# A forgetting attention and a bilinear FFN on one core: the order of issue, the engines of the casts and the buffers laid out anew

## The chip, the core and the metric

The program runs on one core of a Trainium2 chip. A core has five engines with a queue each: PE (TensorE, the matmuls, with its weight loads shown apart as PEld), DVE (VectorE), ACT (ScalarE), POOL (GpSimd) and SP (SyncE, which here only issues transfers). Each engine runs its own list in order and waits by semaphore for what it reads and for the buffers that it writes; 16 DMA engines move what SP, ACT and POOL issue. The metric is the device time of one execution in microseconds. A lower number is better.

## The reference: what is computed

An attention with a decay between tokens, over 8 batches of 8 heads with 576 tokens and 64 features, and then an FFN in which two projections are multiplied:

```python
scores = scale * np.matmul(q, k.transpose(0, 1, 3, 2))
log_f = np.log(np.clip(f, 0.0001, 1.0))
cum = np.cumsum(log_f, axis=-1)
decay = cum[:, :, :, None] - cum[:, :, None, :]
scores = np.where(causal, -1000000000.0, scores + decay)
scores = scores - np.max(scores, axis=-1, keepdims=True)
attn = np.exp(scores)
attn = attn / (np.sum(attn, axis=-1, keepdims=True) + 1e-09)
...
x = np.ascontiguousarray(attn_out.transpose(0, 2, 1, 3)).reshape(B * S, H * D)
...
a = x @ w_a
b = x @ w_b
return (a * b @ w_out).astype(np.float32)
```

All inputs and the output are float32 in DRAM; the kernel multiplies in float16.

## The kernel before

Two heads make a pair, so that there are 32 pairs t, four to a batch. The queries of a pair are cut into blocks i of 128 rows (four, and a last one of 64). For each pair the kernel does this:

- q and k are loaded in halves of a batch (`load_qk`, L339 on SP for batches 1 to 7 into three float32 buffers `n32`, and L334 on POOL's queue for batch 0, where the transfer itself makes float16), cast to float16 (`cast_qk`, lines 291 and 293 on POOL after batch 0), transposed on PE (`pe_transpose`, L359, PSUM tile psT) and copied out to qT and kT (`pe_evict`). v is loaded at L305 (POOL, batches 0 and 1, straight into nv) or L300 (SP, then cast).
- The cumulated logarithm of f is worked out once at the start: two clips (L225, columns 0 to 255 and 256 to 575), two logarithms on ACT (L260), two scans (L228), two casts into a float16 table `crow` (L264), and the low part that float16 loses (`low_part`, L233), one subtraction for each half of the heads. The sums are also stored to DRAM (L238), from where later pairs load them spread over all partitions (L625).
- Scores are matmuls into PSUM tiles sc. In batch 0 the decay is added by matmuls with `crow`, and a row maximum is taken (L646); later it is added on DVE in one pass with the maximum (L674, into S). ACT takes the exponential with its sum (L701, L705, into PA for the blocks 0 to 2 and PB for the rest), DVE the reciprocal (L715 and L713), and POOL or ACT multiplies the rows by it (the normalisation, L726).
- The probabilities are transposed, on PE for batch 0 and partly batch 1 (PSUM tile psP), else by a DMA transpose that SP issues (`do_tr`, L740, PTA from PA and PTB from PB). The product with v (PSUM pv, or pvx from batch 2 on) is copied to xT, the FFN's input.

The FFN takes the tokens in pieces of 256 (three), 384, 512 (six) and 384. A piece is 12 blocks of the inner dimension: matmuls into psa (with w_a) and psb (with w_b), ACT copies psa out to float16, DVE multiplies it with psb into ht (L1073), and for each 128 tokens 24 matmuls with w_out give pso, which ACT or DVE copies to osb and SP stores (L1116). The weights come by POOL's queue (L510): w_a and w_b in a first third and the rest, each in two halves of the partitions, and w_out in three parts. 24 `wake` blocks of matmuls without a use are strewn over the opening.

Nothing schedules this at run time or when it is built. The functions only make a list of 2353 steps (`Op`, with engine, dependencies and the rings of buffers that they take); the long table `ORDER` says in which order the steps are issued, and so the list of each engine; `CHOICE` has one letter for each step that may run on several engines (casts, copies out of PSUM, normalisations), and `SLOTS` says which buffer of its ring each allocation takes. The dependencies of a step become waits on semaphores. Each engine takes its steps strictly in this order, so that a step that waits holds all that stand behind it. Rings around the change: three buffers `n32` for loads, two S, four PA, two PB, three PTA, two PTB, four PSUM banks `ff` (psa, psb, pso, psT, psP, pv) and two `sc` pairs.

Of the kernel before, what the change touches and what calls it, by code (L numbers as in the profile page):

```python
# [25 lines left out]
def kernel(  # L26
# [13 lines left out]
    B, H, S, D = q.shape  # L40
# [22 lines left out]
    qd = [perm.tile([128, 128], FP16, tag=f"qd{i}", name=f"qd{i}") for i in range(2)]  # L63
# [41 lines left out]
    def paddings():  # L105
# [14 lines left out]
    nv = [perm.tile([128, NSB, H, D], FP16, tag=f"nv{i}", name=f"nv{i}") for i in range(2)]  # L120
# [21 lines left out]
        PA:03210213021302130213021302130213;PB:01101010101010101010101010101010;S:010110100110100110101011001101  # L142
        01010101001010101010101010010011010100101001000100010011011010011100111011010101110101;a16:0210210210210
        21021021021021021021201201210210210210201201201012012021021021020120120201010201210201201201201201021;bc
        :0210210210210210210210210210;ff:03120312032100023120310323231232301230103010103203013120312031203120312
        03123012310120213203203013203210312013201320130123021312312031232013012013023103210131310321320312031023
        10210321032130230231023102312302130213021321023023012032032031310210210312310231302132013203210310231023
        20120210102120321312012013203103021301321301302102302310230132031203120132013012012021023101301321032132
        030231031031032031230123201230312312312312312312302311021021302301231231230;ht:0dcba981234567d0bc9a18234
        5670dbc9a182543d670cb9a1428653d70cb2a9154863d7bac025914863dcb7a9205148dc36a9b72051483cdb6;n16:0110100101  # L150
        10001010010101010101;n32:0210201201201201020101212110210220201212202101;nv:01010101;osb:0101010101001010
        10101010010100110101;qd:010101010101010101010101;sc:0101010101010101010101011010010101100010101011001001
        0101101010101011010101010101010100101011101100101010110101100101100100101010;st:054321503421503421503421
        50342150
# [1054 lines left out]
    for n in cuts:  # L1209
# [3 lines left out]
        0 1 29 30 46 2 52 62 5 3 31 37 32 38 33-36 39 40 42 41 53 47 58 4 43 267 262 279 6-9 54 48 10 56  # L1213
# [160 lines left out]
```

## Time and profile before

| what | us |
|---|---|
| median of three runs | 400.78 |
| the three runs | 397.33, 400.78, 401.96 |
| span of the profiled execution | 397.5 |

The profiled execution's span lies by the fastest of the three runs. All times from the trace count from the start of this span. The page lists for each engine its busy time; a window row gives the busy time of each engine within a stretch; a timeline row gives start, length, engine, line, operation, tiles and shapes, and in brackets the idle time ahead of it with what ended it. Idle time of an engine that is not the bottleneck costs nothing by itself.

### The profile page before, as it was taken

What the parts mean: (1) busy time and instruction counts of PE and PEld (TensorE: products, weight loads), DVE (VectorE), ACT (ScalarE), POOL (GpSimd) and SP (SyncE); (2) the same over time, 40 slices, a digit from 0 to 9 for tenths busy, and PEclk for the clock granted to TensorE, in tenths of its full rate; (3) what the DMA queues carried; (4) which work ended last, traced back from release to release, by engine and by line L of the source; (5) the groups of instructions that cost most, each with busy time, mean ns of one, the idle gap of its engine ahead of it and who ended that gap; (6) DMA issues with size and microseconds to landing.
All of it is one profiled execution on the core that took longest, in us unless ns stands there. A gap on an engine that the chain in (4) does not pass through costs nothing.

```text
span 397.5 us, 14691 instructions
## 1 busy us (share of the span) xinstructions
PE 386.4 (97%) x5768; PEld 250.9 (63%) x5768; DVE 293.0 (74%) x971; ACT 290.6 (73%) x805; POOL 257.8 (65%) x464
## 2 busy tenths in 40 slices
PE   6899999999999999999999999999999999999997
PEld 3557887969766665655555665555555556567785
DVE  7888798999998779787888798668878772333131
ACT  5999899999879778778988588898878763232131
POOL 8689687769887679884996877779936871000000
PEclk9999999999999999999999999999999999999999
DMA  7999999999999999999999999999999586100202
GB/s 117 256 195 167 157 147 226 220 285 283 244 188 228 238 293 234 235 249 292 231 205 278 223 255 214 248 258 206 252 220 230 104 147 156 63 2 1 81 28 81
DMA packets 147365, 76.87 MB, mean 193 GB/s; under 512 B 124384, under 2 KB 128352, under 8 KB 147296
## 3 DMA queue, kind: packets, MB, share of 16 engines
q1 hardware_dynamic: 132856, 68.72, 77.7%
q0 software_dynamic: 14256, 7.08, 14.7%
q8 instruction: 45, 0.74, 0.8%
q14 instruction: 24, 0.20, 0.2%
q10 hardware_dynamic: 184, 0.14, 0.1%
HBM read 52.05 MB, written 9.58 MB: 155 GB/s over the span
## 4 chain that ended last, share of the span: by engine, by line
PE 77%; DMA 11%; POOL 4%; ACT 3%; issue 2%; DVE 2%; SPq 0%; DVEq 0%; ACTq 0%; POOLq 0%
PE psa L74 21%; PE psb L74 20%; PE pso L74 20%; PE sc L551 4%; DMA PTA<-PA 3%; PE pvx L769 3%; POOL PA L726 2%; DMA PTB<-PB 2%; PE psT L359 2%; DMA wb<-in_moe_w_b_dram 2%; PE sc L539 2%; DMA wout<-in_q_dram 2%; PE sc L74 1%; PE psP L74 1%; DMA k<-in_k_dram 1%
## 5 line engine op out<-in xcount | busy, mean ns | idle before, releaser
L674 DVE CUSTOM_DVE_ANT_0 S<-sc,spread 64x576 f32<-64x576 f32 (+4 forms) x232 | 125.9, 562 | 17.3 <-ACT PA L705 8.3
L74 PE MATMUL psb<-xT,wb 128*64 128x512 f16 (+2 forms) x1056 | 113.9, 341 | 0.8 <-DMA wb<-in_moe_w_b_dram 0.5
L74 PE MATMUL psa<-xT,wa 128*64 128x512 f16 (+2 forms) x1056 | 114.1, 341 | 0.0
L289 ACT CAST a<-psa 128x512 f16<-128x512 f32 (+1 forms) x114 | 63.3, 559 | 56.4 <-PE psa L74 52.3
L1073 DVE TENSOR_TENSOR ht<-psb,a 128x512 f16<-128x512 f32 (+1 forms) x114 | 74.4, 658 | 38.5 <-PE psb L74 27.7
L74 PE MATMUL pso<-wout,ht 128*64 128x512 f16 x840 | 102.4, 380 | 0.0
L726 POOL TENSOR_SCALAR PA<-PA,st 128x256 f16<-128x256 f16 (+2 forms) x180 | 84.9, 483 | 8.8 <-DVE st L715 5.5
L705 ACT ACTIVATE PA<-S,st 128x256 f16<-128x256 f32 (+2 forms) x168 | 84.2, 504 | 6.5 <-DVE st L674 6.0
L74 PEld LDWEIGHTS <-wb 128*64 128x64 f16 x1056 | 62.5, 110 | 30.0 <-issue 2.5
L74 PEld LDWEIGHTS <-wa 128*64 128x64 f16 x1056 | 61.7, 110 | 29.3 <-issue 2.2
L726 POOL TENSOR_SCALAR PB<-PB,st 128x512 f16<-128x512 f16 (+1 forms) x90 | 63.4, 711 | 24.3 <-DVE st L715 10.7
L74 PEld LDWEIGHTS <-ht 128*64 128x64 f16 x912 | 49.9, 110 | 33.0 <-issue 1.9
L705 ACT ACTIVATE PB<-S,st 128x512 f16<-128x512 f32 x56 | 40.2, 720 | 3.3 <-DVE st L674 3.0
L705 ACT ACTIVATION_READ_ACCUMULATOR PA<-S,st 128x1 f32 x168 | 32.1, 191 | 0.0
L701 ACT ACTIVATE PB<-S,st 128x576 f16<-128x576 f32 x28 | 21.7, 775 | 9.8 <-POOL PA L726 3.1
L631 POOL TENSOR_SCALAR_AFFINE_SELECT spread<-spread 128x768 f32<-128x768 f32 x24 | 20.9, 870 | 10.1 <-DMA spread<-cum_d 10.0
L769 PEld LDWEIGHTS <-nv 128*64 128x64 f16 x640 | 21.7, 110 | 7.5 <-DMA PTA<-PA 2.1
L674 DVE CUSTOM_DVE_ANT_1 S<-sc,spread 128x256 f32<-128x256 f32 x48 | 19.8, 419 | 6.9 <-PE sc L539 2.0
L715 DVE RECIPROCAL st<-st 128x2 f32<-128x2 f32 x128 | 18.3, 156 | 6.9 <-ACT PB L705 3.5
L674 DVE DVE_READ_ACCUMULATOR2_ANT st<- 128x1 f32 (+1 forms) x280 | 23.0, 82 | 0.0
L551 PE MATMUL sc<-kT,qT 64*128 64x512 f16 (+4 forms) x144 | 20.8, 326 | 1.2 <-ACT kT L289 0.4
L289 ACT COPY osb<-pso 128x512 f32<-128x512 f32 x24 | 13.8, 580 | 9.1 <-PE pso L74 7.8
(106 smaller groups left out, 483.2 us busy)
## 6 DMA issues: line engine op xcount, KB each, us to landing
spread<-cum_d SPq DMA_DIRECT2D x24, 576.0 KB, 6.4
out_dram<-osb SPq DMA_DIRECT2D x35, 256.0 KB, 3.4
q<-in_q_dram SPq DMA_DIRECT2D x14, 576.0 KB, 5.7
k<-in_k_dram SPq DMA_DIRECT2D x14, 576.0 KB, 5.0
v<-in_v_dram SPq DMA_DIRECT2D x24, 256.0 KB, 6.0
wout<-in_moe_w_out_dram POOLq DMA_DIRECT2D x3, 512.0 KB, 7.5
nv<-in_v_dram POOLq DMA_DIRECT2D x8, 128.0 KB, 5.1
wa<-in_moe_w_a_dram POOLq DMA_DIRECT2D x2, 512.0 KB, 7.5
```

What stands on the lines that cost most here:

```text
L74: nc.tensor.matmul(out=out[r], lhsT=lhsT[:, r], rhs=rhs, **kw)
L289: nc.scalar.copy(out=out_, in_=in_)
L359: nc.tensor.matmul(out=p[m][HP[j] if quad else slice(0, 128), 64 * t:64 * t + 64], lhsT=x[r, j, t, :] if quad else x[r, t, :], rhs=ident16 ...
L551: nc.tensor.matmul(out=dst, lhsT=lhsT, rhs=rhs, start=start, stop=stop, skip_group_check=True)
L631: nc.gpsimd.affine_select(out=c[:, :, 0:SM].rearrange("p h (j k) -> p h j k", k=128), in_=c[:, :, SM:2 * SM].rearrange("p h (j k) -> p h j ...
L674: nc.vector.tensor_tensor_reduce(out=o, in0=x, in1=y, scale=-1.0, scalar=3e38, op0=ADD, op1=MIN, accum_out=m)
L701: nc.scalar.activation(out=p_blocks(t, 4), in_=T[("s" if direct else "z", t, 4)], func=EXP, bias=st[:, 8:9], scale=sign, accum_out=st[:, 1 ...
L705: nc.scalar.activation(out=p_blocks(t, i)[:, :, h, :], in_=(T[("s", t, i)][:, h, :] if direct else T[("z", t, i)][:, h * n:h * n + n]).rea ...
L715: nc.vector.reciprocal(out=st[:, 20 + 2 * i:22 + 2 * i], in_=st[:, 10 + 2 * i:12 + 2 * i])
L726: VEC[e].tensor_scalar(out=p, in0=p, scalar1=st[:, c:c + 1], scalar2=1.0, op0=MUL, op1=MUL)
L769: nc.tensor.matmul(out=o[HP[h], 128 * i:128 * i + 128], lhsT=vt[:, j, pr + NP * h, :], rhs=pt[:, base_blk[i] + 2 * block_at(t, i, j) + h, ...
L1073: nc.vector.tensor_tensor(out=ht[:, 0:n_], in0=T.pop(("psb", t0, fbs))[:, 0:n_], in1=T.pop(("a16", t0, fbs))[:, 0:n_], op=MUL)
```

## The change

Only the three tables are replaced; the functions that make the steps, the 2353 steps and their dependencies stay. The core of the difference, a line or two of each table:

```diff
     SLOTS = """
-        PA:03210213021302130213021302130213;PB:01101010101010101010101010101010;S:010110100110100110101011001101
+        PA:01230321032103210321032103210321;PB:01101010101010101010101010101010;S:01010110101010101010101100110
...
     ORDER = """
-        0 1 29 30 46 2 52 62 5 3 31 37 32 38 33-36 39 40 42 41 53 47 58 4 43 267 262 279 6-9 54 48 10 56
+        46 2 0 1 29 3 37 31 52 62 5-8 30 38 9 10 32 44 54 56 48 50 33 34 36 35 11 63 53 64 47 4 82 55 65 57 39
...
     CHOICE = """
-        DDDDADADADAAPPAPPPAPPAADAPPPPPPAPADDDDPPPAPPPPPDDDDPAAPAPPPADDDADAADAAAADDPPPAPAPPPADDAAPPAP
+        DDPPADAAADAAPPPPAPPPPDDDDAPPPAPAPPADDDPPPPAPPPPDADAPAPPPAPPPDDDDAAAADAADDPPPPPPPPADDDDAAPAAPPAPAAAAPAA
```

By `CHOICE`, 12 normalisations move from ACT to POOL and nine from POOL to ACT, 11 copies of pso from ACT to DVE and three back, nine copies of psT from DVE to ACT and five back, and the low-part subtractions of the later 320 columns from DVE to POOL.

The list of DVE at the start, where f is prepared, as a piece of the difference (cum_f is f and then the sum, crow the float16 table):

```order
 L93 COPY pick_69<-ident_70 32x32
+L225 TENSOR_SCALAR cum_f<-cum_f 96x320
 L225 TENSOR_SCALAR cum_f<-cum_f 96x256
-L225 TENSOR_SCALAR cum_f<-cum_f 96x320
 L228 SCALAR_TENSOR_TENSOR cum_f<-cum_f,cum_l 96x256
```

The clip of the 320 columns stands first now.

The list of POOL ahead of the paddings, as a piece of the difference (low and neg are masks, wout holds the second half of k of batch 0 for a while, qd is padding):

```order
 L102 AFFINE_SELECT low_62<-low_62 64x128
+L334 DMA wout_78<-in_k_dram 128x2x576
+L233 TENSOR_TENSOR crow<-cum_f,crow 32x320 x2
 L107 MEMSET qd_63 128x128
 L107 MEMSET qd_64 128x128
```

The load of that half of k now follows the masks, and the two subtractions, which DVE did, follow it.

The list of POOL from the last memset of the opening on, before (PA holds probabilities, st the reciprocals, nv is v, spread the spread sums):

```order
L113 MEMSET nv_80 64x512
L726 TENSOR_SCALAR PA<-PA,st 128x128
L621 MEMSET spread_84 128x2x64
L305 DMA nv_79<-in_v_dram 128x8x64 x2
L291 TENSOR_SCALAR q_470<-q_184 128x2x9x64
L726 TENSOR_SCALAR PA<-PA,st 128x2x128
L293 CAST k_473<-k_186 128x2x9x64
```

and now, from the same memset on:

```order
L113 MEMSET nv_80 64x512
L305 DMA nv_79<-in_v_dram 128x8x64 x2
L621 MEMSET spread_84 128x2x64
L305 DMA nv_79<-in_v_dram 128x8x64
L510 DMA wb_77<-in_moe_w_b_dram 64x4x512 x2
L510 DMA wa_76<-in_moe_w_a_dram 64x4x512
L305 DMA nv_79<-in_v_dram 64x8x64
L510 DMA wa_76<-in_moe_w_a_dram 64x4x512
L726 TENSOR_SCALAR PA<-PA,st 128x128
L726 TENSOR_SCALAR PA<-PA,st 128x3x128
L621 MEMSET spread_85 128x2x64
L293 CAST k_554<-k_517 128x2x9x64
```

Four issues of v and four of weights have moved ahead of the first normalisation; the casts of batch 1 stand behind it.

The list of SP at the start, as a piece of the difference (k and q are the float32 loads of batches 1 and 2):

```order
 L213 DMA cum_f<-in_f_dram 32x1x576
+L339 DMA k_517<-in_k_dram 128x2x576
 L238 DMA cum_d<-cum_f 32x576 x2
-L339 DMA q_184<-in_q_dram 128x2x576
-L339 DMA k_186<-in_k_dram 128x2x576
-L339 DMA q_188<-in_q_dram 128x2x576
-L339 DMA k_618<-in_k_dram 128x2x576
-L339 DMA q_620<-in_q_dram 128x2x576
+L339 DMA q_584<-in_q_dram 128x2x576
+L339 DMA q_1096<-in_q_dram 128x2x576
```

The first k load of batch 1 now stands ahead of the store of the sums, and does not wait for them.

The list of POOL further on, around the cast of the first q half of batch 2, which was `q_1303` and is now `q_1653` to `q_1697`; before:

```order
L305 DMA nv_79<-in_v_dram 128x8x64
L291 TENSOR_SCALAR q_1303<-q_620 128x2x9x64
L305 DMA nv_79<-in_v_dram 128x8x64
L305 DMA nv_79<-in_v_dram 64x8x64
L726 TENSOR_SCALAR PB_83<-PB_83,st 128x4x128
```

and now:

```order
L305 DMA nv_80<-in_v_dram 128x8x64
L726 TENSOR_SCALAR PA<-PA,st 128x3x128 x2
L726 TENSOR_SCALAR PA<-PA,st 128x128
L291 TENSOR_SCALAR q_1697<-q_1653 128x2x9x64
L726 TENSOR_SCALAR PB_83<-PB_83,st 128x4x128 x2
L726 TENSOR_SCALAR PA<-PA,st 128x128 x2
L291 TENSOR_SCALAR q_1805<-q_1657 128x2x9x64
```

The cast has moved behind the loads of batch 1's v and the normalisations of pairs 3 to 5.

79 lines of the change are left out of this document (50 added, 29 removed), and 161 rows, old and new, of the table ORDER.

## The prediction

> **What bounds the kernel now.** I read the page first, then the windows by stage, then the list of TensorE's waits, then the timelines of the opening on each engine. The page says that TensorE is the bound:
>
> ```profile
> span 397.5 us, 14691 instructions
> PE 386.4 (97%) x5768; PEld 250.9 (63%) x5768; DVE 293.0 (74%) x971; ACT 290.6 (73%) x805; POOL 257.8 (65%) x464
> ```
>
> TensorE idles 397.5 - 386.4 = 11.1 us in all. The windows (us: TensorE, weight loads, VectorE, ScalarE, GpSimd, then clock, DMA share, GB/s) split the run at the first FFN matmul and at three later points:
>
> ```profile
> 0.00:35.60 35.60, 29.94 (x544) 17.69 (x544) 29.56 (x76) 28.34 (x83) 29.48 (x62) 1.00 0.98 187
> 35.60:121.00 85.40, 84.63 (x1692) 67.33 (x1688) 76.98 (x271) 78.31 (x216) 66.51 (x111) 1.00 1.17 217
> 121.00:175.00 54.00, 52.40 (x748) 33.45 (x744) 44.44 (x160) 43.47 (x127) 43.94 (x78) 1.00 1.14 238
> 175.00:340.00 165.00, 165.00 (x2204) 93.39 (x2202) 124.18 (x440) 125.67 (x352) 117.82 (x216) 1.00 1.02 220
> 340.00:397.50 57.50, 54.47 (x600) 39.05 (x596) 17.80 (x29) 14.80 (x29) 0.00 (x0) 1.00 0.12 43
> ```
>
> The idle time is 5.66 us before the FFN starts, 0.77 us from there to 121 us, 1.60 us to 175 us, none to 340 us, and 3.03 us at the end (the last copy and store). The clock is full throughout. So the time is about: the moment of the first FFN matmul, plus a fixed amount of matmuls, plus some 2.4 us of waits, plus a tail of 3 us. TensorE's waits, longest first:
>
> ```profile
> PE wake L74 <- POOL ident masks.py:199: 2.8, 1, 2.8
> PE pvx L769 <- DMA PTA<-PA: 1.3, 3, 0.8
> PE psT L359 <- DMA wout<-in_q_dram: 0.8, 1, 0.8
> PE psb L74 <- DMA wb<-in_moe_w_b_dram: 0.5, 1, 0.5
> ```
>
> The first is the start of the program. The third is in the opening: q of the second half lands late. The fourth is the second half of w_b, and the second the transposed probabilities of a pair. In the timeline of TensorE, the first FFN matmul, the two places of the later waits, and three transposes of q and k that the steps below need (39.84 and 42.90 of batch 1, 61.70 of batch 2) are these:
>
> ```profile
> 34.13 0.34 PE L769 MATMUL pv<-xT,nv 128*64 128x128 f16 x6
> 34.40 0.39 PE L551 MATMUL sc<-kT,qT 64*128 64x512 f16 x2
> 35.63 1.06 PE L74 MATMUL psa<-xT,wa 128*64 128x256 f16 x16
> 39.84 0.43 PE L359 MATMUL psT<-ident,q 64*128 64x64 f16 x18
> 42.90 0.44 PE L359 MATMUL psT<-ident,k 64*128 64x64 f16 x18
> 45.27 1.06 PE L74 MATMUL psb<-xT,wb 128*64 128x256 f16 x16 [0.46 <-DMA wb<-in_moe_w_b_dram]
> 61.70 0.44 PE L359 MATMUL psT<-ident,q 64*128 64x64 f16 x18
> 172.98 0.36 PE L769 MATMUL pvx<-PTA,nv 128*64 128x128 f16 x6 [0.84 <-DMA PTA<-PA]
> ```
>
> **The change, part by part.** *Fixed work.* No matmul, load, store or elementwise operation is added or removed, so the 386.4 us of busy TensorE stay, but for the 24 wake-up blocks, which fill gaps of the opening and cost nothing as long as the gaps are there. The order of the FFN blocks against the attention's keeps its outline: the first FFN block has as many blocks ahead of it as before. Term: 0.
>
> *The opening.* Three edits meet. First, VectorE clips the 320 columns of f ahead of the 256. The rows of the old order:
>
> ```profile
> 4.54 0.82 DVE L225 TENSOR_SCALAR cum_f<-cum_f 96x256 f32<-96x256 f32 x2 [0.51 <-DMA cum_f<-in_f_dram]
> 5.31 0.69 DVE L228 TENSOR_TENSOR_SCAN cum_f<-cum_f,cum_l 96x256 f32<-96x256 f16 x1
> 8.30 0.32 DVE L264 CAST crow<-cum_f 96x320 f16<-96x320 f32 x1
> 8.66 1.03 DVE L233 TENSOR_TENSOR crow<-cum_f,crow 32x320 f16<-32x320 f32 x2
> ```
>
> The two clips take 0.82 us together, so the one that the first scan needs now ends at about 5.36 instead of 4.83 (0.5 us later), and its logarithm on ScalarE stands behind the other: between 0.5 and 1 us later, I take 0.8. The cast that ended at 8.62 then ends at 9.4.
>
> Second, the two low-part subtractions that follow it move from VectorE to GpSimd, and GpSimd's own list is laid out anew behind them. The rows that price it:
>
> ```profile
> 8.42 0.49 POOL L107 MEMSET qd<- 128x128 f16 x2
> 10.15 0.99 POOL L113 MEMSET nv<- 64x512 f16 x2
> 14.06 0.38 POOL L726 TENSOR_SCALAR PA<-PA,st 128x128 f16<-128x128 f16 x1 [2.92 <-DVE st L715]
> 14.54 1.83 POOL L305 DMA_DIRECT2D nv<-in_v_dram  x2
> 16.39 1.18 POOL L291 TENSOR_SCALAR q<-q 128x1152 f16<-128x1152 f32 x1
> 17.53 0.49 POOL L726 TENSOR_SCALAR PA<-PA,st 128x256 f16<-128x256 f16 x1
> 21.03 0.59 POOL L726 TENSOR_SCALAR PA<-PA,st 128x384 f16<-128x384 f16 x1 [1.48 <-DVE st L715]
> 23.10 0.65 POOL L510 DMA_DIRECT2D wa<-in_moe_w_a_dram  x1
> 33.98 0.68 POOL L726 TENSOR_SCALAR PB<-PB,st 128x512 f16<-128x512 f16 x1
> ```
>
> GpSimd sat idle for 2.92 and 1.48 us there, waiting for reciprocals. Now it issues loads in that time: after the paddings (8.42 to 11.14, so 2.7 us) come four issues of v (3.5 us by 1.83 for two, the half block a little less) and four of weights (2.6 us at 0.65), with a memset of 0.2. From 9.4 on: subtractions 1.0 (at VectorE's 1.03 for both), paddings 2.7, issues 6.3, gives 19.4 for the first normalisation, which was at 14.06. From there to the last normalisation that the second half of pair 2 needs, GpSimd has eight of 128 columns (0.37), six of 256 (0.48), four of 384 (0.58), one of 512 (0.69), two casts (1.16), four weight issues (0.65) and two memsets (0.2): 3.0 + 2.9 + 2.3 + 0.7 + 2.3 + 2.6 + 0.4 = 14.2 us. Starts follow each other some 0.04 us sooner than durations say (17.53 after 16.39 + 1.18), so 13.2 us: 32.6. TensorE then has that transpose (0.34), two PV blocks, one spread and the scores of pair 2 (1.23 from 34.40 to 35.63): 2.2 us, so the first FFN matmul at 34.8, against 35.63 now.
>
> It can wait, since VectorE's reciprocals are also in a new order, and a two-input subtraction has no row on GpSimd. Bounds for the pair: from 0.9 us (0.43 each, the 0.68 us row of 512 columns cut to 320) to 2.4 us (1.18 each, the row of 1152 f32 columns whole). I take 1.5, near the middle and half as much again as on VectorE. That gives 35.3. The Trainium skill, page "GPSIMD Engine Reference", section "4.1 Engine selection", puts two-input elementwise work at about half VectorE's speed on this engine; no run here shows it yet. By that rule the pair takes 2.1 us, and the FFN starts at 35.9.
>
> Third, the first k load of batch 1 is issued on SP right after f, where it stood behind the store of the sums. The loads of batch 0, on GpSimd's queue, were already late at this place:
>
> ```profile
> 9.32 0.48 PE L359 MATMUL psT<-ident,wout 64*64 64x64 f16 x36 [0.83 <-DMA wout<-in_q_dram]
> k<-in_k_dram SPq DMA_DIRECT2D x1, 576.0 KB, 6.1
> 12.00:13.00 1.00, 0.94 (x24) 0.53 (x22) 0.94 (x2) 1.00 (x6) 0.00 (x0) 1.00 1.01 362
> ```
>
> The load brings 576 KB in; at the 362 GB/s of the window in which three such loads ran, it is 1.6 us of all DMA engines, and it lies ahead of or beside the load that TensorE waits for. Between 0 (it slips in ahead of them) and 1.5 us of delay of the first score block; I take 0.8. Only a part reaches the FFN, because GpSimd's list is the longer chain: 0.3. Term of the opening: 35.3 + 0.3 - 35.6 = 0, bounds -0.8 and +1.9.
>
> *The wait for w_b.* The last issue of w_b, in the chain of waits, and one of w_out on POOL:
>
> ```profile
> 37.07 8.06 DMA wb<-in_moe_w_b_dram
> 45.81 0.79 POOL L510 DMA_DIRECT2D wout<-in_moe_w_out_dram  x1
> ```
>
> It was issued at 37.07 and landed 8.06 us later, as TensorE wanted it at 45.27. Now it stands straight ahead of the last normalisation of the sum above, so at about 32, and even at 8 us lands at 40: the 0.46 us wait goes. Term -0.5, bounds -0.5 and 0. Late next at this place are q and k of batch 1. Their second casts stand behind three normalisations, one v and two w_out issues, and then one more normalisation and w_out issue: 33.1 + 2.1 + 0.9 + 1.6 + 1.2 is 39 us, and 0.7 + 0.8 + 1.2 more is 42, where TensorE wants them at 39.84 and 42.90. A miss there gives the 0.5 us back.
>
> *Waits for transposes.* 1.3 us in three places. SP's order around the pairs 9, 11 and 14 keeps both transposes together, with a store or a spread load more or less ahead. I see nothing that lands them sooner by the 0.84 us of pair 14; I take -0.3, bounds -1.3 (all gone) and +1.5 (as many new ones).
>
> *Engine of casts.* Eleven output copies go from ScalarE to VectorE and three back, 12 normalisations from ScalarE to GpSimd and nine back. None lies on TensorE's path from 175 to 340 us, where VectorE and ScalarE have a quarter of their time free and TensorE none: 0, unless one of them is late for a PSUM slot.
>
> *The end.* The last copies and stores are the same: 0.
>
> Sum on the profiled execution: 397.5 + 0 - 0.5 - 0.3 = 396.7. The profiled one is near the fastest of the three runs (397.33); the median, 400.78, lies 3.3 us above it. With TensorE's work fixed, that surplus can only be waits, and the trace shows which kind: transfers that land just as they are wanted. Part of it should stay. I add half, 1.7: **398.4 us**.
>
> **Rivals.** *All waits go.* If the orders meet the transfers so well that the 2.4 us between 35.6 and 175 vanish, the opening gains 0.8 and the surplus stays away, the time is 397.5 - 2.4 - 0.8 = 394.3, and with half the surplus 396. For it: every one of these waits is a transfer, and all weights are issued earlier. Against it: the transposes, the largest, are hardly moved.
>
> *GpSimd is late for batch 2 (slower).* The cast of the first q half of batch 2 was at this row, more than 20 us ahead of its transpose at 61.70:
>
> ```profile
> 40.47 1.14 POOL L291 TENSOR_SCALAR q<-q 128x1152 f16<-128x1152 f32 x1 [1.07 <-issue]
> 49.94 0.69 POOL L726 TENSOR_SCALAR PB<-PB,st 128x512 f16<-128x512 f16 x1 [3.34 <-DVE st L715]
> 60.72 0.20 POOL L621 MEMSET spread<- 128x128 f32 x1 [2.59 <-DVE st L674]
> ```
>
> Now 25 items stand between the opening's last normalisation and it: ten normalisations of 512 or 576 columns (7.1), three of 384 and one of 128 (2.1), five v and three w_out issues (4.4 and 2.4) and three casts (3.5), with its own 1.2 a sum of 20.7 us. From 33.1 us it ends at 53.8 without a wait, and TensorE, which has one FFN block less ahead of it, reaches the transpose at about 60.5. GpSimd's waits in that stretch were 1.07, 3.34 and 2.59 us. If they recur in full (7.0), the cast ends at 60.8, barely late; every further us is one us of idle TensorE, and the cast of the other half and of k follow at once. It decides (over 404.8) from 404.8 - 398.4 = 6.4 us of further delay on: 405 or more. Against it: those waits are where the new order has put other work.
>
> *Nothing changes.* Waits move but do not shrink, the median keeps its surplus: 400.8.
>
> **How the numbers follow.** A measurement of this kernel can tell about 1% from no change, so the bounds are 396.8 and 404.8. Forecast and "nothing changes" both lie within: 0.56 together (0.36 and 0.20). All waits gone, below 396.8: 0.28. Slower, by GpSimd's lateness there or at another cast: 0.16. The range reaches down to the first rival's 394.3 and up to where the second begins to decide: 394.3 to 404.5. Within that, the forecast's own range is 396.5 to 401.
>
> **What would show it.** The first FFN matmul between 34.8 and 37.5 us; no wait of it for w_b; the pair of subtractions on GpSimd near 0.75 us each; waits of pvx for the transposes still near 1 us; the transpose of q of batch 2 without an idle row. A first FFN matmul beyond 38, or TensorE idle before a transpose of q or k, would make the forecast wrong; so would idle TensorE between 175 and 340 us, where there is none now.

## The result, and the profile after

The change made the kernel slower by 0.7%: 402.46 us in the median of 20 runs (400.33 to 409.07) against 399.79 for the kernel before (20 runs, 397.01 to 402.71), a ratio of 1.007 with a 95% interval of 1.0051 to 1.009. That lies within 1%. The time lies inside the predicted range (394.3 to 404.5), but outside the forecast's own range (396.5 to 401) and on the other side of the kernel before.

The head of the page after, the profiled execution being one of 400.98 us:

```profile
span 399.3 us, 14677 instructions
PE 385.8 (97%) x5768; PEld 245.2 (61%) x5768; DVE 291.6 (73%) x971; ACT 287.3 (72%) x800; POOL 259.3 (65%) x469
```

TensorE is busy for 0.6 us less than before (385.8 against 386.4), and the span is 1.8 us longer, so its idle time has grown by 2.4 us. The orders can be compared at two points, since the same blocks of TensorE lie ahead of each in both: the first FFN matmul, and the first pso matmul of the third FFN piece. The windows of the kernel before, cut there, and then those of the kernel after (us: TensorE, weight loads, VectorE, ScalarE, GpSimd, then clock, DMA share, GB/s):

```profile
0.00:35.63 35.63, 29.97 (x544) 17.69 (x544) 29.59 (x76) 28.37 (x83) 29.51 (x62) 1.00 0.98 187
35.63:103.92 68.29, 67.83 (x1444) 56.54 (x1440) 62.17 (x222) 64.87 (x181) 51.87 (x83) 1.00 1.19 216
103.92:397.50 293.58, 288.65 (x3792) 176.68 (x3788) 201.19 (x677) 197.35 (x543) 176.38 (x321) 1.00 0.87 189
```

```profile
0.00:36.60 36.60, 28.98 (x544) 17.27 (x544) 27.21 (x71) 29.05 (x85) 31.77 (x68) 1.00 1.12 212
36.60:105.66 69.06, 67.92 (x1444) 56.75 (x1440) 62.42 (x223) 63.03 (x177) 52.42 (x82) 1.00 1.03 195
105.66:399.30 293.64, 288.86 (x3792) 171.20 (x3788) 201.91 (x680) 195.19 (x540) 175.15 (x321) 1.00 0.84 189
```

The opening takes 0.97 us longer, the stretch behind it 0.77, and the long rest the same to 0.06 us: in this trace the loss is made in the first quarter of the run. TensorE's waits after, longest first:

```profile
PE wake L74 <- POOL ident masks.py:199: 2.8, 1, 2.8
PE psT L359 <- DMA q<-in_q_dram: 1.6, 1, 1.6
PE psP L74 <- POOL PA L726: 1.3, 1, 1.3
PE psb L74 <- issue: 1.1, 1, 1.1
PE psT L359 <- issue: 1.0, 1, 1.0
PE sc L539 <- DVE st L674: 0.9, 1, 0.9
PE sc L551 <- ACT PA L705: 0.8, 2, 0.6
PE psa L74 <- DVE osb L293: 0.3, 1, 0.3
PE pvx L769 <- DMA PTA<-PA: 0.2, 1, 0.2
```

The wait for w_b and most of those for transposes are gone. In their place stand one for q of batch 0, one for a normalisation, one at a score block, two for exponentials, one for an output copy, and two "issue": TensorE waited for nothing that the profile shows. In the timeline of TensorE the new stops, the first FFN matmul, and the two places that the prediction named (psb at 45 us, q of batch 2 at 63 us):

```profile
14.48 0.47 PE L359 MATMUL psT<-ident,wout 64*64 64x64 f16 x35
15.99 0.19 PE L359 MATMUL psT<-ident,wout 64*64 64x64 f16 x1 [1.04 <-issue]
33.11 0.81 PE L74 MATMUL psP<-ident,PA 128*64 128x128 f16 x22 [1.32 <-POOL PA L726]
36.60 1.06 PE L74 MATMUL psa<-xT,wa 128*64 128x256 f16 x16
45.61 0.38 PE L74 MATMUL psb<-xT,wb 128*64 128x256 f16 x4
54.62 0.62 PE L74 MATMUL psb<-xT,wb 128*64 128x256 f16 x7
56.38 0.38 PE L74 MATMUL psb<-xT,wb 128*64 128x256 f16 x3 [1.14 <-issue]
63.37 0.44 PE L359 MATMUL psT<-ident,q 64*128 64x64 f16 x18
141.84 0.40 PE L539 MATMUL sc<-kT,qT 64*128 64x128 f16 x6 [0.92 <-DVE st L674]
```

The stops at 15.99 and 56.38 stand in the middle of a group: 35 of 36 transposes are done, or 7 of 16 matmuls into one PSUM tile, and the next one, which needs nothing new, comes 1 us late. Count TensorE's instructions up to there. The windows from the start to the stop at 56 us, here and, from runs told below, to stops of the same kind in a second execution of this kernel, in the kernel before with one load moved, and in the changed kernel with 144 more instructions at its start:

```profile
0.00:55.20 55.20, 47.58 (x989) 33.85 (x990) 43.74 (x123) 46.23 (x132) 47.23 (x87) 1.00 1.16 206
```

```profile
0.00:51.30 51.30, 42.85 (x861) 29.37 (x862) 39.80 (x102) 41.82 (x118) 43.30 (x82) 1.00 1.14 212
```

```profile
0.00:50.00 50.00, 44.24 (x861) 29.79 (x862) 41.35 (x107) 41.26 (x117) 39.18 (x75) 1.00 1.03 177
```

```profile
0.00:51.30 51.30, 45.57 (x989) 34.47 (x990) 41.08 (x110) 43.12 (x122) 45.03 (x83) 1.00 1.14 214
```

Matmuls and weight loads together are 1979, 1723, 1723 and 1979: the difference is 256. (The expectations below count six more, the queue's own: 449, 1473, 1729, 1985.) The list of DMA queues after has the supply:

```profile
q8 instruction: 45, 0.74, 0.8%
```

45 packets and 0.74 MB make 16 KB each, and TensorE's 11,536 instructions over 45 are 256 a packet. So TensorE's program comes in by DMA, 256 instructions at a time, and it stopped where a packet began. Each packet's transfer takes about 1 us, and what follows runs 1.1 us or more after its end in every trace here. In the trace of after the seventh packet began at 53.91 and ended at 54.80, and TensorE went on at 56.38. (The views don't list single packets; their times are those of queue q8 in the trace's transfer records.) No packet of the two traces begins with more than 303 instructions left, and none of the first eight, up to 58 us, with more than 252. I take one to be asked for at 260; this is an estimate. Here that is 5 us ahead of the stop, and the packet began 4.0 us after it.

### The profile page after: what moved, and what is told of

Its sections match the earlier page's. It is cut to its first block, busy times and chain, and to the rows that moved or that the text cites. A ratio compares the mean times of both kernels' runs of the same rounds, so it can differ in the third digit from the quotient of the medians.

```text
span 399.3 us, 14677 instructions
## 1 busy us (share of the span) xinstructions
PE 385.8 (97%) x5768; PEld 245.2 (61%) x5768; DVE 291.6 (73%) x971; ACT 287.3 (72%) x800; POOL 259.3 (65%) x469
## 4 chain that ended last, share of the span: by engine, by line
PE 84%; ACT 4%; DVE 4%; DMA 4%; issue 2%; POOL 1%; ACTq 0%; DVEq 0%; POOLq 0%
PE pso L74 22%; PE psa L74 21%; PE psb L74 21%; PE sc L551 4%; PE pvx L769 3%; PE psT L359 3%; ACT PA L705 2%; DMA PTB<-PB 2%; PE psP L74 2%; PE sc L539 2%; PE sc L74 2%; DMA q<-in_q_dram 1%; PE wake L74 1%; DVE S L674 1%; PE pv L769 1%
## 5 line engine op out<-in xcount | busy, mean ns | idle before, releaser
L674 DVE CUSTOM_DVE_ANT_0 S<-sc,spread 64x576 f32<-64x576 f32 (+4 forms) x232 | 125.3, 561 | 13.7 <-ACT PA L705 5.0
L74 PE MATMUL pso<-wout,ht 128*64 128x512 f16 x840 | 99.5, 380 | 0.0
L726 POOL TENSOR_SCALAR PA<-PA,st 128x128 f16<-128x128 f16 (+2 forms) x180 | 83.5, 475 | 21.4 <-DVE st L715 13.7
L1073 DVE TENSOR_TENSOR ht<-psb,a 128x512 f16<-128x512 f32 (+1 forms) x114 | 73.6, 657 | 32.4 <-PE psb L74 21.9
L726 POOL TENSOR_SCALAR PB<-PB,st 128x512 f16<-128x512 f16 (+1 forms) x93 | 65.3, 708 | 25.0 <-DVE st L715 13.9
L74 PEld LDWEIGHTS <-wb 128*64 128x64 f16 x1056 | 60.4, 110 | 33.1 <-issue 3.6
L74 PEld LDWEIGHTS <-wa 128*64 128x64 f16 x1056 | 60.0, 110 | 30.6 <-issue 2.2
L293 DVE COPY osb<-pso 128x512 f32<-128x512 f32 x19 | 13.0, 686 | 21.3 <-ACT a L289 8.4
## 6 DMA issues: line engine op xcount, KB each, us to landing
wout<-in_moe_w_out_dram POOLq DMA_DIRECT2D x3, 512.0 KB, 12.2
```

The lines of the kernel that those rows point to most:

```text
L74: nc.tensor.matmul(out=out[r], lhsT=lhsT[:, r], rhs=rhs, **kw)
L293: VEC[e].tensor_copy(out=out_, in_=in_)
L674: nc.vector.tensor_tensor_reduce(out=o, in0=x, in1=y, scale=-1.0, scalar=3e38, op0=ADD, op1=MIN, accum_out=m)
L726: VEC[e].tensor_scalar(out=p, in0=p, scalar1=st[:, c:c + 1], scalar2=1.0, op0=MUL, op1=MUL)
L1073: nc.vector.tensor_tensor(out=ht[:, 0:n_], in0=T.pop(("psb", t0, fbs))[:, 0:n_], in1=T.pop(("a16", t0, fbs))[:, 0:n_], op=MUL)
```

## The experiments

The two theories at the start: "transfers" (the loads that the change issues earlier delay q and the instruction packets) and "order" (the new order of matmuls, rings, norms and GpSimd's list costs the time by semaphore waits). A ratio is always to the kernel before on the same chip. "FFN" is the first FFN matmul and "stretch" the time from it to the third piece; before they are 35.63 and 68.29, after 36.60 and 69.06.

**What the stops are.** The warm-up groups were cut finer, to shift the count:

```diff
-    def wake(n):
+    def wake(n, m=512):
...
-            mm_halves(x, ident16, ident16[:, 0:1].to_broadcast([128, 512]), ...
+            mm_halves(x[:, 0:m], ident16, ident16[:, 0:1].to_broadcast([128, m]), ...
...
-        o = Op("PE", 0.427, lambda _: wake(2), ...
+        o = Op("PE", 0.427, lambda _, n=n: wake(8, 128) if n < 6 else wake(2), ...
```

> The changed kernel with the first six warm-up groups of TensorE cut into four times as many matmuls of a quarter of the columns (72 more matmuls, with their weight loads about 144 more TensorE instructions ahead of everything else, in time in which TensorE waits for q anyway). It changes nothing but where the 256-instruction packets of TensorE's program end. Theory 'transfers' (instruction fetch): every mid-group idle time without a releaser stands at a count of 449 plus a multiple of 256, so the one at 55 us cannot stand before the same matmul: it goes, or stands 144 instructions (3 to 4 us) earlier; the time changes by between -1.3 and +0.5 us against the changed kernel's. Theory 'PSUM or order': the 1.14 us idle stays before the same matmul of the third pair's psb at 55 us, and the time stays within 0.4 us of the changed kernel's.

In the timeline of TensorE of that kernel:

```profile
51.12 0.22 PE L769 MATMUL pv<-xT,nv 128*64 128x128 f16 x1
52.63 0.22 PE L769 MATMUL pv<-xT,nv 128*64 128x128 f16 x1 [1.30 <-issue]
52.77 0.49 PE L74 MATMUL psb<-xT,wb 128*64 128x256 f16 x5
```

The stop stayed at the count of 1979 and left the matmul: it now falls between two of a pv block, ahead of the psb group and not within it. That shows that the stop follows the supply of instructions, and not a PSUM buffer or a semaphore. The time was 402.48 us, ratio 1.0077 (1.0046 to 1.0108): shifting the count wins nothing, since the packet is late wherever its 256 begin.

**The early k load.** Put back in the changed kernel, and made early in the kernel before; on SP's list:

```diff
 L213 DMA cum_f<-in_f_dram 32x1x576
-L339 DMA k_517<-in_k_dram 128x2x576
 L238 DMA cum_d<-cum_f 32x576 x2
 L339 DMA q_584<-in_q_dram 128x2x576
+L339 DMA k_517<-in_k_dram 128x2x576
```

> The changed kernel with one transfer put back: the load of k of batch 1 is queued on SP behind the table's store and the first q load of batch 1, as before the change, instead of second. Theory 'transfers': it alone made q of batch 0 land at 8.6 instead of 6.7 us. q lands at 6.7 to 7.0 again, the transpose of q starts at about 7.1 to 7.6 (cast behind it), the 1.04 us idle before 15.99 goes, the first FFN matmul comes at 35.6 to 36.0 instead of 36.6, and the time is 0.5 to 1.2 us under the changed kernel's (about 1.004 times the kernel before). Theory 'GpSimd's list' (subtractions, norms and casts in another order on GpSimd set the opening): q lands earlier, but the FFN still starts at 36.4 to 36.8 and the time stays at 1.007.

> The kernel before with one transfer moved: the load of k of batch 1 is queued second on SP, as the change has it; nothing else differs. Theory 'transfers': q of batch 0 lands at 8.3 to 8.7 instead of 6.7, the first score block and the FFN move by 0.5 to 1.0 us (first FFN matmul 36.1 to 36.6 instead of 35.6), and the time is 0.4 to 1.1 us over the kernel before (1.001 to 1.003). Theory 'GpSimd's list': q lands later but the FFN stays at 35.5 to 35.9 and the time at 1.000 plus or minus 0.001.

With it back, q of batch 0 landed at 6.71 instead of 8.63 us and the FFN began at 35.96, as the theory wanted; in the order before, q landed at 7.64 instead of 6.70 and the FFN began at 36.19. But the time hardly followed in the first: 401.85 us, 1.0056 (1.0025 to 1.0087); its trace has stops of 1.21 and 0.62 us at the fifth and sixth packets. In the second it did: 400.88 us, 1.0048 (1.0016 to 1.0079), again with a stop, the longest of these, in a kernel whose order is otherwise the old one:

```profile
51.73 0.33 PE L74 MATMUL psP<-ident,PB 128*64 128x128 f16 x5 [1.76 <-issue]
```

**Later loads.** In GpSimd's list two of three w_out loads go behind casts and norms, and three v loads behind the norms of the next pairs:

```diff
-L510 DMA wout_78<-in_moe_w_out_dram 128x4x512 x2
+L510 DMA wout_78<-in_moe_w_out_dram 128x4x512
 L291 TENSOR_SCALAR q_1098<-q_1096 128x2x9x64
 L726 TENSOR_SCALAR PB_82<-PB_82,st 128x576
-L510 DMA wout_78<-in_moe_w_out_dram 128x4x512
 L293 CAST k_1125<-k_1122 128x2x9x64
+L510 DMA wout_78<-in_moe_w_out_dram 128x4x512
...
+L510 DMA wout_78<-in_moe_w_out_dram 128x4x512
```

> The changed kernel with five loads of GpSimd's queue issued later, about where they stood before the change: the second and third of w_out at about 45 and 50 us instead of 38.9 and 41.4, three of v of batch 1 at about 55 to 57 instead of 46 to 48.5. Theory 'transfers' (the 1.14 us idle in the middle of a psb group at 55 us is TensorE out of instructions, because the packet with its next 256 came late behind the crowd): w_out's loads land 7 to 9 us after their issue instead of 12, the packet starts before TensorE's count stands 420 past its 256s, that idle goes, and the time is 0.6 to 1.3 us under the changed kernel's (about 1.004). Theory 'PSUM or order' (the stall is a wait on a buffer that the new ring order makes late, which the page cannot name): the stall stays at the same matmul, 0.8 us or more, and the time stays within 0.4 us of 1.007.

The median time from issue to landing of w_out's loads, 12.2 us after, fell to 8.0; the packet asked for at 50 us began 1.1 us later instead of 4.0, and the stop at 56 us went. The stretch was 68.34 us, that of the kernel before; the FFN stayed at 36.42. The time: 401.20 us, 1.0053 (1.0024 to 1.0083), an interval that overlaps the changed kernel's, so that the trace shows the stop gone and the time only suggests a gain. The opposite, a transfer added in the order before:

```diff
             o.fn(o.eng)
+            if o.n == 278:
+                nc.sync.dma_start(out=crowd, in_=T[("T", "k", 1)].rearrange("p a s -> p (a s)"))
```

> The kernel before with one transfer added that nothing waits for: SyncE, idle there, copies the finished k tile of batch 1 (590 KB) to a spare array in DRAM at about 46 us. All other instructions and their order are those of the kernel before. Theory 'transfers' (instruction fetch): the packet of instructions that is asked for at 43 or at 50 us starts 1 to 3 us later than without it, TensorE stops at a count of 1729 or 1985 for 0.3 to 2 us with no releaser, and the time rises by 0.3 to 2 us (1.001 to 1.005). Rival: more traffic only delays w_out's loads, TensorE's packets keep their 2 to 3 us of wait, no stall without a releaser shows, and the time is 1.000 plus or minus 0.001.

The rival was right: 590 KB more at 46 us left the packet asked for at 50 us at 3.1 us (3.2 before) and the time at 399.44 us, 1.0011 (0.9977 to 1.0044). What the transfer delayed were w_out's loads (9.1 us in the median, 7.5 before); TensorE waited 0.93 us for one at 57 us. So these bytes did not make this packet late. They came too late for the packet asked for at 43 us, which began at 44.7 us, and in the changed kernel it is that one, too, that comes late.

Then all early transfers were put back, in two steps:

> The changed kernel with the transfers of 23 to 56 us thinned out: the later issue of w_out's second and third load and of three v loads of batch 1 (as in the run with loads moved back), and besides the first k load of batch 2 goes from 23 us to behind the store at 60 us, where it stood before the change, with its cast after the other cast of batch 2; the first q load of batch 2 takes the buffer that this leaves and is issued at about 24 us instead of 41. The early k load of batch 1 stays. Theory 'transfers': fewer transfers stand in front of the packets with TensorE's next 256 instructions; no mid-group idle over 0.5 us at 449 plus a multiple of 256 after 20 us, w_out's loads land 7 to 9 us after issue, and the time is 1.000 to 1.004 times the kernel before (the run with loads moved back alone measured 1.0053). Theory 'order': the loss is in the matmul order and rings; the time stays at 1.005 to 1.008.

> The same thinned-out transfers, and the early k load of batch 1 back behind the store and the first q load, so that all transfers that the change put ahead stand about where they were; the order of matmuls, casts, norms and rings is the changed kernel's. Theory 'transfers': the opening is 0.5 to 0.7 us earlier than in the thinned-out kernel (first FFN matmul 35.8 to 36.1), no instruction stall over 0.5 us, and what the new order saves (the waits ahead of two pvx groups at 137 and 171 us and the w_b wait, together 1.8 us in the trace of before) shows: 0.995 to 1.002 times the kernel before. Theory 'order': 1.004 to 1.008.

Both missed: 407.88 us (1.0199) and 407.16 us (1.0196). One edit of mine was the main reason: a v load of batch 1 came to stand on GpSimd behind a cast that waited, and TensorE waited 3.1 and 2.9 us for v at 77 us. The windows of the first of the two show a second price (the clock stands third from the end):

```profile
74.00:76.00 2.00, 0.28 (x6) 0.17 (x6) 0.12 (x1) 1.82 (x5) 0.32 (x1) 1.00 1.12 387
76.00:78.00 2.00, 0.52 (x8) 0.47 (x10) 1.55 (x9) 2.00 (x7) 0.74 (x1) 0.83 1.32 244
78.00:80.00 2.00, 2.00 (x24) 1.65 (x20) 1.43 (x8) 0.81 (x5) 1.50 (x2) 0.50 0.84 152
80.00:82.00 2.00, 2.00 (x38) 1.89 (x36) 0.58 (x3) 0.87 (x2) 1.51 (x5) 0.82 1.24 167
```

Behind the idle time the granted clock fell to half, by the three windows for 3.4 us (0.17, 0.50 and 0.18 of full speed lost, twice that at half, each over 2 us). With that load in front:

> The two kernels with thinned-out transfers lost 3.1 us at 74 us to a load of mine: the fourth v load of batch 1 stood on GpSimd behind the k cast of batch 2, which waited. Here that load is issued before the casts of batch 2 and the k cast stands two norms further ahead; otherwise it is the kernel with both sets of transfers back (order of matmuls, rings, norms and casts the changed kernel's). Theory 'transfers': FFN at 35.7 to 36.0, idle for instructions under 0.8 us in all before 60 us, no wait for v at 74 us, and 0.996 to 1.003 times the kernel before. Theory 'order': 1.005 to 1.008.

402.82 us, 1.0101 (1.0077 to 1.0126). The wait for v went, and between 20 and 60 us no stop for instructions was over 0.3 us. But there is one of 1.8 us at the very first packet (16.3 us, FFN 36.91), so that the expectation for the opening missed, and behind the FFN's start the kernel was no better: its stretch is 69.55 us. "Transfers" as the whole cause has fallen.

**GpSimd's two subtractions.** They went back to VectorE:

> The kernel with all transfers back, and the last two subtractions of the decay table on VectorE again instead of GpSimd. The theory that GpSimd's list costs the rest of the opening: GpSimd comes 1.6 us earlier to its first loads and norms, and the first FFN matmul moves from about 36.0 to 35.5 to 35.8; the time falls by 0.2 to 0.6 us against the kernel with them on GpSimd. The theory that their place doesn't matter: the two kernels agree within 0.3 us, and the FFN starts within 0.15 us of the other's.

> The kernel with all transfers back, and besides the last two subtractions of the table on VectorE, this time right behind the two they belong to, as before the change (in the earlier run they stood behind two evictions, and the FFN came 3.1 us late). Theory 'GpSimd's list': the first FFN matmul comes 0.1 to 0.5 us before that of the kernel with all transfers back and the time falls by as much. Theory 'their engine costs nothing': the first FFN matmul within 0.1 us, the time within 0.3 us of it.

The first builds on the second of the kernels that wait for v at 77 us (1.9 us here). Its subtractions stood behind two row maxima (L646; the expectation calls them evictions), TensorE waited 1.2 us for them, its clock fell to half from 13.7 to 20.5 us, and the FFN came at 38.95: 405.05 us, 1.0150. In the second, in their old place, the FFN came at 35.31. The kernel it was to be compared with has its stop of 1.8 us ahead of the FFN; against the one before that, whose opening is the same but for the subtractions (35.82), it is 0.5 us, as the theory had it. With the 0.64 us of the early k load this is the whole 1.1 us by which the change moved the FFN. But the time did not come back with it: 402.41 us, 1.0088 (1.005 to 1.0127), against 1.0101 with overlapping intervals, and above the changed kernel's 1.007.

**Chance or order.** Both kernels once more:

> The changed kernel itself once more, for a second trace of it. If the packets of instructions are late because of what the kernel itself transfers there, the stalls at the counts 449 and 1985 show again (0.7 us idle or more at one of them at least); if they were chance of one execution, neither shows.

> The changed kernel a third time. First FFN matmul at 36.3 to 36.7, the wait of 1.3 us at 32 and that of 1 us at 140 us again, since they follow from the order; instruction stalls of 1 to 3 us in all before 60 us if they belong to the changed order (its two traces have 2.6 and 3.8 by the count), and anything from 0 to 3 us if they are chance.

> The kernel before once more, for a second trace. If the instruction stalls of 36 to 56 us belong to the changed order, it has none over 0.5 us, as in its first trace; if they come from one execution to the next in either order, one may stand at a count of 1473, 1729 or 1985 here too, and the trace is then 0.7 to 2.5 us longer than the first (397.5).

The second trace of before has FFN 35.21, stretch 68.36 and no stop between 20 and 60 us, like the first. The further two of after have FFN 36.41 and 38.05, stretch 70.46 and 72.21, and idle time for instructions between 36 and 60 us of 1.7 and 2.7 us (1.1 in the first). The expectation for the second trace, 0.7 us or more at the count of 449 or 1985, missed: those two are 0.2 us each, and the stops stand at the fifth and sixth packets. So their place varies from one execution to the next. They are in all three traces of the changed kernel and in neither of the kernel before, but they are not the changed order's alone: the two kernels of the old order with a single load moved have 1.8 us each (the early k load above, and w_b below). The waits at 32 us (1.3) and 140 us (0.9) are in all three. The last one shows the clock again, in the windows from 8 us, where TensorE waited 1.3 us for q and 0.3 us for the next load:

```profile
8.00:10.00 2.00, 0.87 (x38) 0.79 (x40) 0.51 (x2) 0.36 (x1) 1.85 (x4) 1.00 1.14 200
10.00:12.00 2.00, 1.68 (x50) 1.05 (x48) 0.00 (x0) 1.35 (x3) 1.78 (x8) 0.71 1.08 192
12.00:14.00 2.00, 2.00 (x40) 1.41 (x38) 1.10 (x3) 1.60 (x5) 1.94 (x5) 0.50 1.07 362
14.00:16.00 2.00, 2.00 (x32) 0.78 (x30) 1.64 (x2) 2.00 (x11) 1.96 (x5) 0.94 1.31 276
```

This execution took 406.48 us. The clock fell a second time at the end of the stop of 2.14 us that ended at 48.55. Of the changed kernel's 22 runs in all, 8 had a mean clock of 0.996 or less; of the 100 of the kernel before beside the experiments, 5; of the kernel before with the early k load, 5 of 12; of the changed kernel with that load back, none of 12. Of the other kernels of the changed order that don't wait for v at 77 us, those that keep the early load have 3 of 39 such runs, those without it none of 25. So in these runs the lower clock goes with the early load, but the early load alone does not bring it, and the kernels ran on several chips.

**Two waits of the order.** A norm of the first pair, which stood ahead of those that TensorE waits for at 32 us, and the eviction that the change gave to VectorE:

```diff
-L726 TENSOR_SCALAR PB_82<-PB_82,st 128x4x128
 L726 TENSOR_SCALAR PA<-PA,st 128x2x128
 L726 TENSOR_SCALAR PA<-PA,st 128x128
+L726 TENSOR_SCALAR PB_82<-PB_82,st 128x4x128
```

> The changed kernel with one norm moved on GpSimd: the 512-column one of the first pair (0.7 us, needed only later) behind the two 384-column parts of the fourth pair, for which TensorE waits 1.3 us at 32 us in every trace of the changed order. Theory 'two waits': the wait shortens by 0.6 to 0.8 us, the first FFN matmul comes at 35.7 to 36.1 instead of 36.4 to 36.6, and the time falls by 0.4 to 0.8 us against the changed kernel's (1.004 to 1.006). Theory 'only the instruction stalls differ': the wait shortens, and the time stays at 1.006 to 1.008.

> The changed kernel with one eviction put back: the second half of the first k eviction of batch 4 on ScalarE right behind the first half, as before the change, instead of on VectorE behind a decay step. Theory 'two waits': the 1.0 us idle in the middle of a score block at 140 us goes, and the time falls by 0.6 to 1.0 us (1.004 to 1.006). Rival: the wait goes, but the next one in the chain (a wait for an exponential or a pvx group within 20 us) takes over at least half of it, and the time stays within 0.4 us of the changed kernel's.

The first shortened its wait from 1.32 to 0.67 us (with a new one of 0.37 behind it), and the kernel was slower: 403.54 us, 1.0119 (1.0084 to 1.0154). Its trace has late loads of batch 0, the halved clock from 17 to 20.5 us and FFN 38.90, so that it doesn't price the norm. The second cut the wait at 140 us from 0.92 to 0.26 us; 401.45 us, 1.0059 (1.0035 to 1.0083), by the ratios 0.4 us under the changed kernel, with overlapping intervals. So the wait is the eviction's, and theory and rival are not told apart.

**The gain that was promised.** The w_b load alone, in the order before:

> The kernel before with one load moved: the last load of w_b directly behind the one before it on GpSimd, three norms earlier. It prices by itself the term of my sum that the change should gain there. Theory of the sum: it lands about 1.5 us earlier, the 0.65 us wait of the psb group at 45 us goes, the time falls by 0.3 to 0.6 us (0.9985 to 0.9993 times before). Theory 'transfers': the wait goes, but the other transfers of 35 to 50 us land later by as much or a packet of instructions is late, and the time stays within 0.2 us of before.

The wait for w_b went, and the time stayed: 399.79 us, 1.0014 (0.9987 to 1.0041). Its trace has instead "issue" of 0.5 us at the fifth packet and 1.3 at the sixth. That is as much as in the changed kernel (1.1 to 2.7), and yet this kernel is not measurably slower than the kernel before: a stop in a trace is no loss of the same size in time either.

**All parts together.**

> The changed kernel with four parts undone together: the k load of batch 1 behind the store and the first q load; w_out's second and third load and three v loads of batch 1 later; the last two subtractions of the table on VectorE right behind theirs; the k eviction of batch 4 on ScalarE. The k load of batch 2 stays where the change put it. Theory 'these parts': first q at 6.5 to 7.4 us, FFN at 35.2 to 35.9, no instruction stall over 1 us at 36 to 60 us, no 1 us wait at 140 us, and 0.999 to 1.003 times the kernel before (undone singly, the parts measured 0.0014, 0.0017, about 0.0013 and 0.0011 of the time). Theory 'the rest of the order' (matmuls, rings, norms): the waits go and others take their place; 1.004 to 1.007.

> The kernel before with the change's early transfers only: the k load of batch 1 second on SP, the three w_out loads at about 39 us one behind the other, three v loads of batch 1 at about 48. Order of matmuls, rings, casts and norms is that of the kernel before. Theory 'these parts': q at 7.6 to 8.7, FFN at 36.0 to 36.4, instruction stalls of 1 to 3.5 us at 36 to 60 us, 1.004 to 1.008. Theory 'the rest of the order': 1.002 to 1.005, no more than with the early k load alone (1.0048, 1.0016 to 1.0079).

The first missed, 401.32 us, 1.005 (1.0027 to 1.0074), where its rival "the rest of the order" had 1.004 to 1.007. Its trace has FFN 35.02, earlier than that of the kernel before, no wait at 140 us and a span of 398.0; but the stretch is 69.73 us, with 1.0 us of idle time for instructions and 0.3 for a norm. Its interval overlaps the changed kernel's, so that 0.8 us regained, by the ratios, is only the best estimate; the parts undone singly had measured 0.0055 of the time together, 2.2 us, and so do not add up. The second, 411.98 us (1.0285), does not answer: w_out's loads, put ahead, held back a v load of batch 0 behind them, TensorE waited 6.1 us for it, and the clock halved. Its FFN came at 39.62 already. TensorE waited 1.70 us for q at 8.95 us, and eight wake matmuls at 10.04 us took 1.92 us there, where eight at 7.42 us take 1.06 in the trace of before: by the spacing of these matmuls (0.42 us, then 0.21) TensorE ran at half speed up to 15.4 us, where the clock column still says 1.00.

No kernel tried here beats the kernel before.

## Why the prediction was wrong

Two steps failed. The opening, put at 0, cost 1.1 us, and the stretch behind it, where waits were to go, cost 0.8 to 2.1 us, with 1.1 to 1.7 us of stops for instructions, which had no term in the sum.

*The base.* I took the span, 397.5 us, for the profiled execution's time and called the median's 3.3 us above it waits. An execution takes 1.7 us more than its span (399.18 against 397.5, 400.98 against 399.3). The 1.7 us of "half the surplus" that I added were just these, for a wrong reason; by luck the base came within 0.6 us of the median before (399.2 against 399.79), and the error lies in the terms: -0.8 us promised, +2.7 us measured.

*The opening, "0, bounds -0.8 and +1.9": this step failed, in its size.* In traces with a full clock the first FFN matmul moved from 35.63 and 35.21 to 36.60 and 36.41, by 1.1 us. Of its parts, the clips cost less than the 0.8 taken, and the pair of subtractions was near the 1.5, as the rows of VectorE and GpSimd after show:

```profile
8.47 0.32 DVE L264 CAST crow<-cum_f 96x320 f16<-96x320 f32 x1
8.95 1.64 POOL L233 TENSOR_TENSOR crow<-cum_f,crow 32x320 f16<-32x320 f32 x2 [0.58 <-issue]
33.69 0.59 POOL L726 TENSOR_SCALAR PA<-PA,st 128x384 f16<-128x384 f16 x1
```

The cast ended at 8.79 instead of 8.62 (9.4 predicted). The last normalisation of the sum ended at 34.28 instead of 33.1 (32.6 in the sum, and 0.5 more for the subtractions): GpSimd waited on the way (0.77 us for an exponential ahead of 19.81, 0.85 us for a reciprocal ahead of 31.01), which I had named and put at nothing. From there to the FFN it was 2.3 us (2.2 in the sum). And the early k load delayed q by 1.9 us, not 0.8; undoing it moved the FFN by 0.64 us and doing it in the order before by 0.56 or more, where I had 0.3. The Trainium skill, page "GPSIMD Engine Reference", section "4.1 Engine selection", has such work at about half VectorE's speed, by which I estimated 2.1 us; here it was 1.64 against 1.03, 1.6 times as long. Undone, the opening's loss did not return as time: with the FFN at 35.31 and at 35.02, earlier than before the change, the kernels still measured 1.0088 and 1.005, because the stretch behind grew. So "the moment of the first FFN matmul plus a fixed amount" failed as a sum, too: its terms are not independent.

*w_b, -0.5.* Right in the trace, the wait is gone. In time, the single edit measured +0.4 us by the medians, with -0.5 us just at the edge of its interval, so that the gain is not shown.

*Transposes, -0.3.* The waits fell from 1.3 to 0.2 us in the first trace. In the second trace of before they are 2.6 us, so that one trace doesn't size them. I had looked for waits near 1 us to stay; they shrank more than I took, and the time was lost elsewhere.

*Casts' engines, "0, unless one of them is late for a PSUM slot".* One was: the eviction at 140 us moved to VectorE, behind a decay step that waited 1.21 us, and held a score block for 0.92 us. I had looked for cover only from 175 us on, and there, too, an output copy, now on VectorE, held up an FFN matmul:

```profile
181.07 0.69 DVE L293 COPY osb<-pso 128x512 f32<-128x512 f32 x1
181.81 1.05 PE L74 MATMUL psa<-xT,wa 128*64 128x512 f16 x8 [0.25 <-DVE osb L293]
```

Between 175 and 340 us TensorE idled 0.43 us, where it had idled none in both traces of before. The prediction had named this as a sign of being wrong; it came, though small.

*What had no term.* "The moment of the first FFN matmul, plus a fixed amount of matmuls, plus some 2.4 us of waits" leaves out that TensorE's program itself is a transfer. Loads issued earlier, which the prediction counts as a gain, share the DMA engines with its packets; between 36 and 60 us TensorE uses up 256 instructions in 5 to 7 us, and a packet begins 0 to 5.7 us after it is asked for by the estimate above. The kernel before just gets by there: its packets end 1.78 us or more ahead of their use in both traces, where TensorE's stops stand at 1.1 to 1.7. The changed order does not. The Trainium skill, page "Runtime: NRT & Kernel Launch", section "Instruction fetch mechanics", has the blocks of 256 instructions on a DMA queue of their own, and says that the cost of crossing to the next one is mostly hidden; the trace agrees on the blocks, and here 1.1 to 2.7 us of it showed.

*The rival that was to make it slower* did not come: the transpose of q of batch 2 stands at 63.37 without an idle row.

*What stays open.* The runs show the places (opening +1.1 us, the stretch to the third piece +0.8 to +2.1, the rest nothing) and three mechanisms: q behind the early load, late instruction packets, and a halved clock behind idle time in some executions. How the 2.7 us divide among them is not shown. Undone together, the parts returned about 0.8 of 2.7 us; the rest lies in what they leave in place, the order of matmuls, buffers and normalisations, which no run here takes apart. Why the packet asked for at 44 us still begins 3.2 to 4.5 us later in every kernel of the changed order, later loads or not (2.7 and 1.3 us in the traces of before, but 5.7 and 5.0 in two kernels of the old order with one load moved), when 590 KB more in the order before did not delay the one that they met, is not settled; whether it is the form or the queue of the transfers was not tried.

## What to carry to other kernels

An order that is planned by loads and waits alone can lose to the transfers that the plan leaves out: look in the trace for idle time in the middle of a matmul group, count the instructions up to it, and if the counts differ by multiples of 256, it is the program that is late. Issuing a load earlier was not free ahead of the first load that TensorE waits for, and where TensorE runs short instructions it can go with late packets. And a wait of 0.5 us that goes from a trace is not yet 0.5 us of time, nor is an earlier FFN: price it by a kernel with that edit alone.

## What the runs showed of the hardware

- TensorE's instructions come in packets of 256 (16 KB); a packet takes 0.9 to 2.3 us, and TensorE goes on no sooner than 1.1 us after its end. Stops of 0.2 to 2.1 us at counts 256 apart stand in kernels of both orders.
- A stop of 2.14 us, or two of 1.30 and 0.32 us close together, were followed by half the granted clock, each time for 3.4 us by the windows (0.71, 0.50, 0.94 above; 0.59 and 0.55 from 48 us on); other stops of 1.3 to 1.8 us were not. The Trainium skill, page "TensorE: Matmul & The Clock Gate", section "Part 1: The HAM clock gate", has windows of 3.4 us, and the length agrees; it asks for a whole idle window, and here less idle time sufficed, in some executions and not in others.
- Two subtractions of 32x320, with two inputs each, took 1.64 us on GpSimd and 1.03 us on VectorE.
